# Batch 0 of an attention and expert kernel: float32 probabilities, joint weight scales, other priorities

## The chip, the cores and the metric

The kernel runs on one core of a Trainium2 chip. The metric is device time in microseconds (us), as the median of the runs. A core has five engines that work side by side, each through its own instructions in a fixed order: TensorE (PE, matmuls; the loads of its stationary operand are listed as PEld), VectorE (DVE), ScalarE (ACT), GpSimd (POOL) and SyncE (SP), which here only issues DMA transfers. They wait for each other by semaphores.

## The reference

Causal attention over 4 batches of 12 heads, 448 positions of 64 columns, and behind it an expert layer whose hidden values are the largest of three products:

```python
scores = scale * np.matmul(q, k.transpose(0, 1, 3, 2))
scores = np.where(mask, -1000000000.0, scores)
scores = scores - np.max(scores, axis=-1, keepdims=True)
attn = np.exp(scores)
attn = attn / (np.sum(attn, axis=-1, keepdims=True) + 1e-09)
attn_out = np.matmul(attn, v)
x = attn_out.transpose(0, 2, 1, 3).reshape(1792, 768)
h = np.maximum(np.maximum(x @ w1, x @ w2), x @ w3)
out = h @ w_out
```

All four weight matrices are 768 x 768 and arrive in float64; q, k and v are float32.

## The kernel before, in words

**Number formats.** Expert and output products run in float16 with each operand split in two parts, a high one (the value rounded) and a low one (what is left): three matmuls, high x high, high x low, low x high, stand for one in higher precision. Splitting costs a copy for the high part and a subtraction for the low part (`scaled`, `rest`, `scaled_rest`, lines 306 to 331, so that many rows of the profile carry L308, L312, L319 or L328).

**Attention** goes by pairs of heads, six to a batch, 24 in all (`attend`, line 432). A pair has two halves of blocks. For each half TensorE computes masked scores into PSUM (tile S, line 449, in float32), VectorE takes maxima (L476), ScalarE exponentiates with a running sum (L487) into tile p. Then ScalarE adds a small number to the sums (L496), VectorE takes reciprocals (L499), ScalarE multiplies every block by its reciprocal (L308, p<-p), makes the high part (L308, ph<-p), and VectorE or GpSimd the low part (L319). A DMA transposes both parts to tile pT (L549), issued by SP. For the first pair alone (`ON_PE = 1`) TensorE transposes instead (L517), and ScalarE and VectorE copy the two parts out of PSUM. The product with v is 60 float16 matmuls into tile O (L569), which ScalarE or VectorE and VectorE split into x (L308 or L310, L328).

**Values** (line 362): v of a batch is loaded to tiles vr, its largest absolute value found (L378 or L376), spread over partitions by a matmul against the identity and a maximum (`all_max`, L344 and L347), and v scaled by a power of two into high and low part.

**Weights** (line 593): 24 tiles, three (one of each of w1, w2, w3) for each of six slices f, and six of w_out. A tile is loaded into one of two staging buffers wst (L603). ScalarE takes the absolute value of the high words (L634), VectorE clamps and takes the maximum (L619), and puts the float64 bits together as float32 in three steps (L623, L627, L631). A power of two as its scale comes from a chain of its own: L344 on TensorE, then L347, L644, L649, L357, L657 on VectorE. With it the tile is split into high and low part (L308 or L312, L328). For each f the ratios of the three scales are found (L675 to L677); when the last tile's scale is known, tile wu (L685).

**Experts** (lines 701 and 752): for batch b and slice f, 54 float16 matmuls (L715), whose three results VectorE and ScalarE bring to a common scale and take the largest of (L308, L729); then the projection (L761) and the output.

**Order.** The instructions are not issued as the functions are written. Each function adds operations with a cost, the names that they read and write, a ring of buffers and a priority to a planner (`Order`, line 54). It plays the program through with the costs and puts each operation on an engine where it can start first, by priority among those ready, and the code is issued in that sequence. Pair u has priority 10 u, weight tile m priority 10 W_AT[m] + 5, the experts 5000 and up. The table `ENGINES` says which engines may take a kind of operation, `RINGS` how many buffers each kind has. What the planner gives is a fixed order on each engine.

Of the kernel before, what the change touches and what calls it, by code (L numbers as in the profile page):

```python
# [30 lines left out]
W_AT = [2.0, 2.3, 2.6, 2.9, 3.2, 3.5, 3.8, 4.1, 4.4, 4.7, 5.0, 5.3, 5.6, 5.9, 6.2, 6.5, 6.8, 7.1, 8.0, 8.3, 8.6, 8.9, 9.2, 9.5]  # L31
V_AHEAD = 2

ON_PE = 1
ENGINES = {
    "q": ("pool", "act"), "v max": ("act",), "v hi": ("act", "pool"), "v lo": ("dve", "pool"), "p": ("act",),
    "p hi": ("act",), "p lo": ("dve", "pool"), "t hi": ("act",), "x hi": ("act", "dve"),
# [4 lines left out]
    qr=3, kr=3, acc=2, p32=2, ph=3, pT=2, v16=5, vr=4, x=4, wst=2, w3=2, h=6, hacc=4, osb=2, S=2, O=1, M=3)  # L42
# [214 lines left out]
def attention_moe(ctx: ExitStack, tc: tile.TileContext, q, k, v, w1, w2, w3, wo, out):  # L257
# [9 lines left out]
        pT=([P, 16, P], F16), v16=([P, 2, DM], F16), vr=([P, DM], F32), x=([P, 3, 2, S_LEN], F16), wst=([P, 3072], F16),  # L267
        w3=([P, DM], F32), h=([P, 2, S_LEN], F16), hacc=([P, S_LEN], F32), osb=([P, HF], F32))
# [5 lines left out]
    tiny = c1.tile([P, 1], F32, name="tiny")  # L274
# [6 lines left out]
    oscL = c1.tile([P, 1], F32, name="oscL")  # L281
    osc = c1.tile([P, 4], F32, name="osc")
# [8 lines left out]
    wx = c1.tile([P, 24], F32, name="wx")  # L291
# [67 lines left out]

    VROWS = [(j, P if j < 3 else 64) for j in range(4)]  # L360

    def values(b, prio):

        s, name = bsc[:, b], ("scale", b)
        for j, n in VROWS:
            t = ("vr", b, j)

            def ld(e, j=j, t=t, n=n):
                ENG[e].dma_start(T(t)[0:n], v[b, P * j : P * j + n, :])

            add(c_dma((n, 3072)), ld, writes=[t], ring=("vr", t), prio=prio)


            def sm(e, j=j, t=t, n=n):
                if e == "act":
                    ACT.activation(junk[0:n, 0:DM], T(t)[0:n], AF.Abs, accum_out=s[0:n, j : j + 1])  # L376
                else:
                    DVE.tensor_reduce(  # L378
                        out=s[0:n, j : j + 1], in_=T(t)[0:n], op=ALU.max, axis=AX.X, apply_absolute_value=True)

            c = dict(act=c_act(DM, 0.09), dve=c_dve(DM))
            add([(e, c[e]) for e in (("dve",) if b == 0 else ENGINES["v max"])], sm, reads=[t], writes=[("sum", b, j)], prio=prio)
# [9 lines left out]
        f = s[:, 10:11]  # L392
        for j, n in VROWS:
            t, v16 = ("vr", b, j), ("v16", b, j)
            first = b == 0 and j == 3
# [36 lines left out]
    def attend(b, p, prio, on_pe):  # L432
# [4 lines left out]
        for z, blocks in enumerate(HALVES):  # L437
# [56 lines left out]

            def eps(e, cols=cols):
                ACT.activation(cols(14), cols(7), AF.Identity, bias=tiny, scale=1.0 / PS)  # L496
# [12 lines left out]

            if on_pe:  # L510

                for g in range(2):
                    M, t = ("M", "t", b, p, z, g), pT[z]

                    def tr(e, g=g, M=M, y=y):
                        for i in range(4):
                            PE.transpose(T(M)[:, i * P : i * P + P], T(y)[:, (4 * g + i) * P : (4 * g + i + 1) * P], ident)  # L517

                    def place(t, g, pl):
                        return T(t)[:, 8 * pl + 4 * g : 8 * pl + 4 * g + 4].rearrange("p a b -> p (a b)")  # L520

                    def t_hi(e, g=g, M=M, t=t):
                        scaled(e, place(t, g, 0), T(M)[:, 0:512], 1.0)

                    def t_lo(e, g=g, M=M, t=t):
                        rest(e, place(t, g, 1), T(M)[:, 0:512], place(t, g, 0))

                    own = [(y, bl[0]) for bl in blocks if any(512 * g <= bl[3] + 512 * k < 512 * g + 512 for k in range(bl[2]))]
                    add([("pe", 0.5)], tr, reads=own, writes=[M], ring=("M", M), prio=pr + 0.4)
                    c = dict(act=c_act(512), dve=c_dve(512))  # L530
                    add([(e, c[e]) for e in ENGINES["t hi"]], t_hi, reads=[M], writes=[(t, 0, g)],
                        ring=("pT", t) if g == 0 else None, prio=pr + 0.4, bank=M, chain=t)
                    add([("dve", c["dve"])], t_lo, reads=[M, (t, 0, g)], writes=[(t, 1, g)], prio=pr + 0.4, bank=M)
                continue
# [25 lines left out]
        def pv(e):  # L560
# [11 lines left out]

        vb = [(("v16", b, j), z) for j in range(4) for z in range(2)]
        add([("pe", 3 * c_pe(*(6 * [P] + 4 * [D])) + 0.3)], pv, reads=[(pT[z], pl, g) for z in range(2) for pl in range(2) for g in range(2)] + vb, writes=[O],
            ring=("O", O), prio=prio + 0.9)
        x, kx = ("x", b, p // 3), p % 3
        fx = 1.0 / PS

        def x_hi(e):
            scaled(e, T(x)[:, kx, 0], T(O)[:, 0:S_LEN], fx)  # L580
# [12 lines left out]
    def weight(m, prio):  # L593
# [234 lines left out]
    for m in range(24):  # L828
        weight(m, 10 * W_AT[m] + 5)
# [39 lines left out]
```

## Time and profile before

| | |
|---|---|
| median of 3 runs | 527.47 us (527.2 to 531.83) |
| the profiled execution: span from first to last instruction | 525.1 us |
| TensorE busy in it | 477.4 us, 91% |
| VectorE, ScalarE, GpSimd busy | 308.1, 318.7, 116.7 us |
| 16 DMA engines, mean share | 52.7% of the span, 65.03 MB |

The profile is of one execution, for which the span is given; the runs of the median were timed without it. [...] The granted clock is given as a share of full speed.

### The profile page before, as it was taken

How to read it: one execution, taken by the hardware profiler on the slowest of the kernel's cores; microseconds unless marked ns; L12 is line 12 of the kernel's file. 1: busy time of each engine (PE TensorE's matmuls, PEld its weight loads, DVE VectorE, ACT ScalarE, POOL GpSimd, SP SyncE). 2: the span in 40 equal slices, each digit the busy share in tenths (PEclk: the TensorE clock that was granted, in tenths of full speed). 3: DMA queues.
4: the chain of work that ended last, by engine and by line, in shares of the span. 5: the costliest groups of instructions: out<-in, count | busy, mean ns of one | idle time of the engine just before them, and what ended most of it. 6: DMA issues, size and time to landing. Idle time of an engine off the chain costs nothing.

```text
span 525.1 us, 9862 instructions
## 1 busy us (share of the span) xinstructions
PE 477.4 (91%) x3826; PEld 279.3 (53%) x3826; DVE 308.1 (59%) x609; ACT 318.7 (61%) x768; POOL 116.7 (22%) x115
## 2 busy tenths in 40 slices
PE   6767554799999999998999999999999999999996
PEld 3445433446555555554665556665555555555563
DVE  5889998999999997995556856333212200212200
ACT  3999688778979879589999797582110111110111
POOL 3432334515556556030021210000000000000000
PEclk9766857799999999999999999999999999999999
DMA  7787797876987998843787840665200011000012
GB/s 233 216 227 180 163 250 205 248 166 169 223 166 212 205 195 176 230 83 79 159 177 145 147 81 12 133 150 104 48 0 1 1 45 46 0 1 0 1 62 60
DMA packets 127599, 65.66 MB, mean 125 GB/s; under 512 B 101440, under 2 KB 124992, under 8 KB 127552
## 3 DMA queue, kind: packets, MB, share of 16 engines
q1 hardware_dynamic: 127552, 65.03, 52.7%
q8 instruction: 30, 0.49, 0.4%
q14 instruction: 17, 0.14, 0.1%
HBM read 35.39 MB, written 5.51 MB: 78 GB/s over the span
## 4 chain that ended last, share of the span: by engine, by line
PE 55%; DVE 21%; ACT 15%; DMA 6%; issue 3%; SPq 0%; ACTq 0%; DVEq 0%
PE M L715 31%; PE M L761 13%; PE S L449 7%; ACT p L487 3%; ACT p L308 3%; DVE w L627 3%; PE O L569 3%; DVE acc L476 2%; ACT ph L308 2%; DVE w L619 2%; ACT w L308 2%; DMA vr<-in_v_dram 2%; DVE w L631 2%; DMA wst<-in_moe_w_dram 2%; ACT w L634 2%
## 5 line engine op out<-in xcount | busy, mean ns | idle before, releaser
L715 PE MATMUL M<-x,w 128*128 128x448 f16 x1296 | 254.7, 355 | 0.0
L715 PEld LDWEIGHTS <-w 128*128 128x128 f16 x1296 | 125.4, 98 | 118.0 <-issue 6.3
L729 DVE SCALAR_TENSOR_TENSOR hacc<-M,wr,hacc 128x448 f32<-128x448 f32 x48 | 32.7, 681 | 105.5 <-PE M L715 105.5
L487 ACT ACTIVATE p<-S,acc 128x384 f32<-128x384 f32 (+3 forms) x168 | 82.9, 500 | 16.2 <-DVE acc L476 7.6
L308 ACT ACTIVATE p<-p,acc 128x384 f32<-128x384 f32 (+3 forms) x168 | 78.1, 531 | 17.4 <-DVE acc L499 16.9
L449 PE MATMUL S<-kr,qr 64*128 64x384 f32 (+4 forms) x384 | 74.9, 446 | 0.0
L761 PE MATMUL M<-w,h 128*128 128x384 f16 x432 | 72.1, 326 | 0.0
L476 DVE TENSOR_REDUCE acc<-S 128x2 f32<-128x512 f32 (+2 forms) x96 | 62.3, 680 | 15.9 <-PE S L449 15.6
L319 POOL TENSOR_TENSOR ph<-p,ph 128x1024 f16<-128x1024 f32 x25 | 56.6, 2266 | 63.2 <-ACT ph L308 46.7
L308 ACT ACTIVATE h<-hacc 128x448 f16<-128x448 f32 x24 | 13.6, 577 | 72.4 <-DVE hacc L729 72.3
L449 PEld LDWEIGHTS S<-kr,qr 64*128 64x128 f32 (+1 forms) x384 | 45.2, 211 | 21.9 <-issue 14.8
L761 PEld LDWEIGHTS <-h 128*128 128x128 f16 x432 | 41.6, 98 | 28.5 <-issue 1.0
L745 POOL COPY hL<-h 128x128 f16<-128x128 f16 x24 | 9.7, 407 | 208.0 <-DVE h L319 207.8
L308 ACT ACTIVATE ph<-p 128x1024 f16<-128x1024 f32 x46 | 48.3, 1051 | 0.5 <-DMA pT<-ph 0.3
L569 PEld LDWEIGHTS <-v 128*64 128x64 f16 x1440 | 39.1, 119 | 10.8 <-issue 10.5
L569 PE MATMUL O<-pT,v 128*64 128x128 f16 (+1 forms) x1440 | 41.9, 221 | 2.7 <-DMA pT<-ph 2.7
L319 DVE TENSOR_TENSOR ph<-p,ph 128x1024 f16<-128x1024 f32 x21 | 25.7, 1222 | 17.0 <-ACT ph L308 15.0
L449 PE MATMUL S<-mk,identb 128*128 128x128 bf16 (+1 forms) x120 | 19.2, 263 | 17.0 <-ACT p L487 10.7
L487 ACT ACTIVATION_READ_ACCUMULATOR p<-S,acc 128x1 f32 x168 | 34.2, 204 | 0.0
L308 ACT ACTIVATE osb<-M,osc 128x384 f32<-128x384 f32 x22 | 12.8, 580 | 30.6 <-PE M L761 30.5
L308 ACT ACTIVATE hacc<-M,wr 128x448 f32<-128x448 f32 x24 | 15.2, 634 | 26.4 <-PE M L715 26.4
L344 PE MATMUL M<-ident,wmx 128*128 128x128 f32 x48 | 13.1, 360 | 17.7 <-DVE w L619 17.7
(79 smaller groups left out, 410.5 us busy)
## 6 DMA issues: line engine op xcount, KB each, us to landing
wst<-in_moe_w_dram SPq DMA_DIRECT2D x18, 768.0 KB, 5.0
kr<-in_k_dram SPq DMA_DIRECT2D x24, 224.0 KB, 3.3
qr<-in_q_dram SPq DMA_DIRECT2D x24, 192.0 KB, 3.7
vr<-in_v_dram SPq DMA_DIRECT2D x12, 384.0 KB, 4.8
wst<-in_moe_w_out_dram SPq DMA_DIRECT2D x6, 768.0 KB, 5.7
out_dram<-osb SPq DMA_DIRECT2D x24, 192.0 KB, 1.9
qr<-in_q_dram SPq DMA_DIRECT2D x48, 16.0 KB, 3.3
vr<-in_v_dram SPq DMA_DIRECT2D x4, 192.0 KB, 4.9
```

Of the source, the lines that this page charges most:

```text
L308: ACT.activation(o, i, AF.Copy, scale=f)
L319: ENG[eng].tensor_tensor(out=o, in0=i, in1=hi, op=ALU.subtract)
L344: PE.matmul(T(M)[:, i * P : i * P + P], ap(c, 0, [[0, P]]), ident, start=True, stop=True)
L449: PE.matmul(o[:, c : c + w], l, r, start=start, stop=True, skip_group_check=True)
L476: DVE.tensor_reduce(out=T(acc)[:, at : at + len(g)], in_=i, op=ALU.max, axis=AX.XY if parts == 2 else AX.X, negate=True)
L487: ACT.activation(part(T(y), parts, c, w), part(T(S), parts, c, w), AF.Exp, bias=T(acc)[:, at : at + 1], accum_out=T(acc)[:, 7 + at : 8 + at])
L569: PE.matmul(T(O)[D * h : D * h + D, P * i : P * i + w], vt[j][:, vl, (2 * p + h) * D : (2 * p + h + 1) * D], T(pT[u])[:, 8 * pl + c, a : a ...
L619: DVE.tensor_scalar(out=T(x32), in0=T(x32), scalar1=MIN_HI, scalar2=None, op0=ALU.max, op1=ALU.max, accum_out=wmx[:, c])
L627: DVE.scalar_tensor_tensor(out=xi(), in0=word(0), scalar=29, in1=xi(), op0=ALU.logical_shift_right, op1=ALU.bitwise_or)
L715: PE.matmul(T(M)[:, 0:S_LEN], w16[j][:, kk, wl, fs], xx[:, kk % 3, xl], start=(kk == 0 and wl + xl == 0), stop=(kk == 5 and wl == 1))
L729: DVE.scalar_tensor_tensor(out=a, in0=ps, scalar=r, in1=a, op0=ALU.mult, op1=ALU.max)
L761: PE.matmul(T(M)[:, 0:HF], lhs(f, hl), w16[3][:, f, wl, es], start=(f == 0 and hl + wl == 0), stop=(f == 5 and hl == 1))
```

## The change

**Batch 0 in float32** (`PLAIN = 6`, all pairs of batch 0). v of batch 0 is loaded as float32 straight into the buffers of the two float16 parts and not split. For its six pairs the exponentials stay as they are: no normalization, no split. TensorE transposes them in float32 (four groups of four transposes), ScalarE or VectorE copies each group from PSUM to pT. The product with v is 20 float32 matmuls. The reciprocals of the sums are spread over the head's 64 partitions by eight matmuls against the identity into one of the three PSUM tiles M, copied with v's scale to a tile of the ring hacc, and the product is multiplied by them on VectorE (line 623 of the new code); then x is split. The transposes by DMA remain for batches 1 to 3.

**Scales.** For three weight tiles there is one chain: three matmuls side by side in one tile M, one maximum with three results, and four small steps on three columns.

**Priorities and tables.** W_AT has other numbers; the maxima of v of batch 0 may go to ScalarE or VectorE, the low part of x of batch 0 to VectorE or GpSimd, the copies to pT and of the reciprocals to ScalarE or VectorE.

```diff
-W_AT = [2.0, 2.3, 2.6, ..., 9.2, 9.5]
+W_AT = [1.0, 1.2, 1.39, ..., 6.13, 6.32]
-ON_PE = 1
+PLAIN = 6
+FIRST = 1
...
+            if plain:
+                for g in range(2):
+                    M, t = ("M", "t", b, p, z, g), pT[z]
+                    def tr(e, g=g, M=M, y=y):
+                        for i in range(4):
+                            PE.transpose(T(M)[:, i * P : i * P + P], T(y)[:, (4 * g + i) * P : (4 * g + i + 1) * P], ident)
+                    def place(e, g=g, M=M, t=t):
+                        scaled(e, raw(t)[:, 512 * g : 512 * g + 512], T(M)[:, 0:512], 1.0)
...
+                continue
...
+        def pv_plain(e):
+            vt = [raw(("v16", b, j)) for j in range(4)]
...
+                        PE.matmul(
+                            T(O)[D * h : D * h + D, P * i : P * i + w], vt[j][:, (2 * p + h) * D : (2 * p + h + 1) * D],
+                            raw(pT[u])[:, a : a + w], start=n_ == 0, stop=n_ == len(per[0]) - 1)
...
+            def reciprocals(e):
+                a = T(acc)
+                DVE.tensor_scalar(out=a[:, 14:21], in0=a[:, 7:14], scalar1=1e-9, scalar2=None, op0=ALU.add)
+                DVE.reciprocal(a[:, 21:28], a[:, 14:21])
+            def spread(e):
...
+                        PE.matmul(
+                            T(R)[D * h : D * h + D, P * i : P * i + P], ap(a, 21 + (2, 4, 0)[i] + h, [[0, D]]), ident,
+                            start=True, stop=True)
...
+            def quotient(e):
+                DVE.tensor_tensor(out=T(x32), in0=T(O)[:, 0:S_LEN], in1=T(x32), op=ALU.mult)
...
-        all_max(("wt", m), [wmx[:, c]], pm, [("wmx", m)], [("wt", m)], prio)
...
+    def scales(f, prio):
+        c, names = slice(3 * f, 3 * f + 3), [("wt", 3 * f + z) for z in range(3)]
+        pm, tt, ff = wpm[:, c], wt[:, c], wf[:, c]
+        all_max(("wt", f, "all"), [wmx[:, 3 * f + z : 3 * f + z + 1] for z in range(3)], pm, [("wmx", 3 * f + z) for z in range(3)],
+                names, prio)
...
-            attend(b, p, 10 * u + 2, u < ON_PE)
+            attend(b, p, 10 * u + 2, u < PLAIN)
...
-    for m in range(24):
-        weight(m, 10 * W_AT[m] + 5)
+    for f in range(8):
+        for m in range(3 * f, 3 * f + 3):
+            weight(m, 10 * W_AT[m] + 5)
+        scales(f, 10 * W_AT[3 * f + 2] + 5)
+        for m in range(3 * f, 3 * f + 3):
+            split(m, 10 * W_AT[m] + 5)
```

**What the planner makes of it.** On VectorE, during batch 0, one weight tile's own scale chain before (w_91 and w_92 are buffers of weights, wpm, wx, wt and wf the columns of the scale, S_105 scores of the next half):

```order
L328 SCALAR_TENSOR_TENSOR w_0_111<-w_91,wf,w_0_111 128x6x128
L627 SCALAR_TENSOR_TENSOR w_92<-wst_90,w_92 128x768
L347 TENSOR_REDUCE wpm<-M_108 128x1
L476 TENSOR_REDUCE acc_68<-S_105 128x2
L644 TENSOR_SCALAR wx<-wpm 128x1
L649 SCALAR_TENSOR_TENSOR wt<-wpm,wx 128x1
L357 TENSOR_SCALAR wt<-wt 128x1
L657 RECIPROCAL wf<-wt 128x1
```

and the first joint chain in the new order (acc_67 holds the sums and reciprocals of a pair, w_87 is the third tile of the group):

```order
L347 TENSOR_REDUCE wpm<-M_111 128x3
L689 SCALAR_TENSOR_TENSOR w_87<-wst_92,w_87 128x768
L712 TENSOR_SCALAR wt<-wpm 128x3
L693 SCALAR_TENSOR_TENSOR w_87<-wst_92,w_87 128x768
L354 TENSOR_SCALAR wt<-wt 128x3
L608 TENSOR_SCALAR acc_67<-acc_67 128x7
L609 RECIPROCAL acc_67<-acc_67 128x7
L357 TENSOR_SCALAR wt<-wt 128x3
L497 TENSOR_REDUCE acc_68<-S_106 128x2
L719 RECIPROCAL wf<-wt 128x3
```

The five steps stand once for three tiles, with three columns each, between the same bit steps and score maxima.

On ScalarE, the end of the second pair of batch 0 before (p_69 and p_70 are the halves' exponentials, ph their float16 parts):

```order
L308 ACTIVATE p_69<-p_69,acc_68 128x384 x2
L308 ACTIVATE p_69<-p_69,acc_68 128x128 x2
L308 ACTIVATE p_70<-p_70,acc_68 128x256
L308 ACTIVATE ph_71<-p_69 128x1024
L308 ACTIVATE p_70<-p_70,acc_68 128x256
L308 ACTIVATE p_70<-p_70,acc_68 128x2x256
L308 ACTIVATE x_85<-O_107 128x448
L308 ACTIVATE ph_72<-p_70 128x1024
```

and the same pair in the new order (M_109 to M_111 are PSUM tiles with transposed probabilities or, into hacc, spread reciprocals):

```order
L508 ACTIVATE p_70,acc_68<-S_107,acc_68 128x256 x2
L308 ACTIVATE x_88<-hacc_100 128x448
L508 ACTIVATE p_70,acc_68<-S_107,acc_68 128x2x256
L308 ACTIVATE pT_74<-M_109 128x512
L395 ACTIVATE junk,bsc<-vr_81 128x768
L308 ACTIVATE pT_75<-M_110 128x512
L308 ACTIVATE pT_75<-M_109 128x512
L308 ACTIVATE hacc_101<-M_111,bsc 128x448
```

The normalizations and the float16 parts are gone, and copies out of PSUM stand in their place.

On SP, the transfers about the second and third pair before:

```order
L603 DMA wst_89<-in_moe_w_dram 128x6x256
L549 DMA_TRANSPOSE pT_74<-ph_71 128x16x128
L549 DMA_TRANSPOSE pT_75<-ph_72 128x16x128
L423 DMA kr_66<-in_k_dram 128x448
L418 DMA qr_63<-in_q_dram 128x384
L420 DMA qr_63<-in_q_dram 64x64 x2
```

and in the new order:

```order
L665 DMA wst_92<-in_moe_w_dram 128x6x256
L376 DMA vr_84<-in_v_dram 64x768
L444 DMA kr_66<-in_k_dram 128x448
L439 DMA qr_63<-in_q_dram 128x384
L441 DMA qr_63<-in_q_dram 64x64 x2
L665 DMA wst_93<-in_moe_w_dram 128x6x256
```

No transposes stand between the loads of batch 0; the first is for the first pair of batch 1.

## Rows read from the trace of the kernel before

**Rows 1.** Chain of work that ended last: start, length, what.

```profile
262.60 0.68 ACT p L487 x2
...
439.40 57.89 PE M L715 x306
497.29 23.41 PE M L761 x144
```

**Rows 2.** Page, 40 slices: granted clock of TensorE in tenths.

```profile
PEclk9766857799999999999999999999999999999999
```

**Rows 3.** Windows: stretch, length; busy PE, PEld, DVE, ACT, POOL; clock, DMA share, GB/s.

```profile
0.00:99.70 99.70, 63.66 (x582) 42.34 (x582) 86.46 (x191) 77.10 (x200) 36.32 (x44) 0.74 0.81 212
99.70:232.20 132.50, 127.17 (x1056) 73.18 (x1057) 125.14 (x261) 110.35 (x262) 61.69 (x42) 0.97 0.81 192
...
23.00:26.40 3.40, 3.28 (x26) 2.04 (x26) 3.40 (x7) 3.40 (x12) 0.00 (x0) 0.50 0.79 206
```

**Rows 4.** Timeline of VectorE, and one piece of GpSimd's: start, length, what.

```profile
22.75 2.85 DVE L328 SCALAR_TENSOR_TENSOR v<-vr,bsc,v 128x768 f16<-128x768 f32 x3
...
30.31 0.62 DVE L328 SCALAR_TENSOR_TENSOR x<-O,x 128x448 f16<-128x448 f32 x1
...
99.68 0.61 DVE L328 SCALAR_TENSOR_TENSOR x<-O,x 128x448 f16<-128x448 f32 x1
...
101.08 6.62 DVE L328 SCALAR_TENSOR_TENSOR v<-vr,bsc,v 128x768 f16<-128x768 f32 x3
...
101.69 5.21 POOL L319 TENSOR_TENSOR ph<-p,ph 128x1024 f16<-128x1024 f32 x2 [0.38 <-ACT ph L308]
...
232.11 1.20 DVE L685 TENSOR_TENSOR wu<-wt,wtm 128x6 f32<-128x6 f32 x1
```

**Rows 5.** Groups by line: engine, operation, tiles, shapes, count; busy, mean ns; idle.

```profile
L347 DVE TENSOR_REDUCE wpm<-M 128x1 f32<-128x128 f32 x24 | 6.8, 281 | 0.9 <-PE M L344 0.8
L644 DVE TENSOR_SCALAR wx<-wpm 128x1 int32<-128x1 int32 x24 | 3.5, 144 | 0.1
L649 DVE SCALAR_TENSOR_TENSOR wt<-wpm,wx 128x1 int32<-128x1 int32 x24 | 11.8, 493 | 0.1
L357 DVE TENSOR_SCALAR wt<-wt 128x1 f32<-128x1 f32 x24 | 3.5, 147 | 0.2
L657 DVE RECIPROCAL wf<-wt 128x1 f32<-128x1 f32 x24 | 3.8, 156 | 0.1
...
L619 DVE TENSOR_SCALAR_CACHE_REDUCE w<-w 128x768 f32<-128x768 f32 x24 | 22.7, 946 | 5.4 <-ACT w L634 5.4
L623 DVE TENSOR_SCALAR w<-w 128x768 int32<-128x768 int32 x24 | 14.5, 602 | 0.0
L631 DVE SCALAR_TENSOR_TENSOR w<-wst,w 128x768 int32<-128x768 int32 x24 | 23.5, 977 | 0.0
L328 DVE SCALAR_TENSOR_TENSOR w<-w,wf,w 128x768 f16<-128x768 f32 x24 | 24.3, 1011 | 1.0 <-ACT w L308 1.0
...
L319 DVE TENSOR_TENSOR ph<-p,ph 128x1024 f16<-128x1024 f32 x21 | 25.7, 1222 | 17.0 <-ACT ph L308 15.0 <-issue 2.0
L328 DVE SCALAR_TENSOR_TENSOR v<-vr,bsc,v 128x768 f16<-128x768 f32 x11 | 13.1, 1210 | 1.0 <-POOL v L312 1.0
L378 DVE TENSOR_REDUCE bsc<-vr 128x1 f32<-128x768 f32 x3 | 2.8, 949 | 5.0 <-DMA vr<-in_v_dram 5.0
...
L308 ACT ACTIVATE p<-p,acc 128x384 f32<-128x384 f32 (+3 forms) x168 | 78.1, 531 | 17.4 <-DVE acc L499 16.9
L308 ACT ACTIVATE ph<-p 128x1024 f16<-128x1024 f32 x46 | 48.3, 1051 | 0.5 <-DMA pT<-ph 0.3
```

**Rows 6.** Timeline of TensorE: start, length, what.

```profile
16.77 1.62 PE L517 MATMUL M<-ident,p 128*128 128x128 f32 x12
...
279.26 1.57 PE L569 MATMUL O<-pT,v 128*64 128x128 f16 x60
...
281.09 1.14 PE L449 MATMUL S<-kr,qr 64*128 64x384 f32 x8
```

More of the change, by code (lines that the diff above doesn't have):

```diff
@@ L392, in values @@
         f = s[:, 10:11]
+        if plain(b):
+            return
         for j, n in VROWS:
             t, v16 = ("vr", b, j), ("v16", b, j)
-            first = b == 0 and j == 3
+            first = b == FIRST and j == 3
             if first:
@@ L508, in attend @@
                     port=True)
[L510 to L534, printed above, removed]
             def p_hi(e, z=z, y=y):
@@ L579, in x_hi @@
+        add([("pe", 3 * c_pe(*(6 * [P] + 4 * [D])) + 0.3)], pv, reads=pb + vb, writes=[O],
+            ring=("O", O), prio=prio + 0.9)
         def x_hi(e):
@@ new lines, in scales, with ratios @@
+        add([("dve", 0.15)], lambda e: exponent(tt, tt), writes=names, prio=prio)
+        add([("dve", 0.15)], lambda e: at_least(tt, 2.0**-62), writes=names, prio=prio)
+        add([("dve", 0.15)], lambda e: DVE.reciprocal(ff, tt), reads=names, writes=[("wf", 3 * f + z) for z in range(3)], prio=prio)
+        if f < KC:
+            def ratios(e):
+                DVE.tensor_reduce(out=wtm[:, f : f + 1], in_=tt, op=ALU.max, axis=AX.X)
+                DVE.reciprocal(wtm[:, 6 + f : 7 + f], wtm[:, f : f + 1])
+                DVE.tensor_scalar(
+                    out=wr[:, c], in0=tt, scalar1=wtm[:, 6 + f : 7 + f], scalar2=2.0**-18, op0=ALU.mult, op1=ALU.mult)
+            add([("dve", 0.5)], ratios, reads=names, writes=[("wr", f), ("wtm", f)], prio=prio + 1)
@@ L659, in place, with split @@
+    def split(m, prio):
+        x32, ff = ("w32", m), wf[:, m : m + 1]
+        f, j = divmod(m, 3) if m < 18 else (m - 18, 3)
         def place(hl):
@@ L670, in weight @@
             reads=[("wf", m), ("w", m, 0)], writes=[x32, ("w", m)], prio=prio, port=True)
-        if m < 18 and j == 2:
-            t3 = wt[:, 3 * f : 3 * f + 3]
-            def ratios(e):
-                DVE.tensor_reduce(out=wtm[:, f : f + 1], in_=t3, op=ALU.max, axis=AX.X)
-                DVE.reciprocal(wtm[:, 6 + f : 7 + f], wtm[:, f : f + 1])
-                DVE.tensor_scalar(
-                    out=wr[:, 3 * f : 3 * f + 3], in0=t3, scalar1=wtm[:, 6 + f : 7 + f], scalar2=2.0**-18,
-                    op0=ALU.mult, op1=ALU.mult)
-            add([("dve", 0.5)], ratios, reads=[("wt", m - z) for z in range(3)], writes=[("wr", f), ("wtm", f)], prio=prio)
         if m == 23:
```

98 lines of the change are left out of this document (68 added, 30 removed).

## Prediction

> **What bounds the kernel now.** I read the profile from the end backwards. In the chain of work that ended last the last piece of another engine that matters is ScalarE's at 262.60 us; behind it stand only scores, products, expert matmuls and projections, at the end two pieces of 57.89 and 23.41 us [rows 1]. So the last half is TensorE's own work, and only an earlier beginning helps. The page's line of the granted clock says where TensorE is not full: in the first quarter slices lie below full speed [rows 2]. The windows show the same by stage [rows 3]: up to 99.7 us TensorE is busy 63.66 us at a mean clock of 0.74, while VectorE is busy 86.46 of 99.7 us; then 127.17 of 132.5 us, beside VectorE at 125.14.
>
> What ends the first stage is VectorE. Its timeline shows the last x of batch 0 written at 99.68 us [rows 4]; only then can the 1296 expert matmuls run on, since each sums over all twelve heads. VectorE stays the second bound until 232.11 us, where the last weight's scale is known (tile wu).
>
> So the time is: start of the experts, plus a rest of TensorE's work that the change leaves alone (the order before and after has the scores of eight pairs of heads and six products with v ahead of the first expert matmul, and all else behind it), plus what the weights hold it up. I predict the shift of the start and of the wu instruction.
>
> **The change part by part.** The base is the profiled execution's span, 525.1 us; the median of the runs is 527.47, 2.4 more, and I add the gain to that.
>
> *VectorE up to the last x of batch 0.* Summed along its own order with the mean durations of this trace, VectorE has 101.1 us of instructions there before and 71.2 after. The pieces, from [rows 5]:
> - Scales: nine chains of 281 + 144 + 493 + 147 + 156 = 1221 ns (11.0 us) become two chains for three tiles each. The maximum over 384 columns is not in the trace; between 281 ns for 128 and 946 for 768 I put it at 547, and the four small ones at 147 each: 1.1 us a chain, 2.3 in all. Saved 8.7.
> - The low parts of the probabilities: four on VectorE at 1222 ns, saved 4.9. The low parts of v of batch 0: four at 1210, saved 4.8. Three maxima of v at 949 go to ScalarE: 2.8.
> - Added: per pair two reciprocal steps and one product, less the old reciprocals and the old x: 0.3 together.
> - Not saved but moved behind the start: the four steps of one weight (946 + 602 + twice 977), two low parts of weights (2 x 1011), a low part of v, a set of ratios and two maxima of scores, about 9.
>
> Together -30. Before, the 74.2 us of durations between the first pair's x (30.31) and the last (99.68) took 69.4 us, a factor 0.935, as neighbours overlap a little. After, pair 0 should end near 21 us (scores, four exponentials, transposes, product in a chain) with 13.2 us of durations done, and 58.0 are left: 21 + 0.935 x 58.0 = 75.
>
> *VectorE from there to wu.* The sums are 139.1 before, which took 132.4 us (0.952), and 142.9 after, as the moved 9 us come back and the remaining chains are cheaper. With 136 us the wu instruction falls 136 us behind the start.
>
> *TensorE in the first stage.* 47 us at full clock (63.66 x 0.74) stand there now, an upper bound as latency counts as busy. Added for five pairs are 16 transposes: twelve took 1.62 us [rows 6], so 0.135 each, 2.16 a pair. The product with v in float32 has 20 matmuls, 2048 columns over both heads. The float32 scores of 1024 such columns took 1.14 us [rows 6], so 2.3 us; spreading the reciprocals, 896 columns, 1.0 us; the 1.57 us of the float16 product goes. That is 3.9 a pair, less the transposes that pair 0 has already: 6 x 3.9 - 2.2 = 21 us. No row shows float32 with 64-column weights. From below: if its columns cost what those of the float16 product do, a third of 1.57 and 0.2, the sum is 6 us. From above: if the two heads don't run beside each other, twice the price, 41 us. I take 21, the float32 row being the nearest. The hidden stage then needs 68 us at full clock.
>
> *ScalarE.* Per pair of batch 0 it loses seven normalizations at 531 ns, two high parts at 1051 and two small ones (some 6.4 us), and gets about 3.3 copies of 512 columns, one of the spread reciprocals and a maximum of v, at 531 to 949 each: some 3.5 to 4.5. It was busy 77.10 of 99.7 us; about 65 remain. With VectorE at 71 and TensorE at 68 three engines are now loaded nearly alike, and each waits in order for the others. For that I add 6 us to VectorE's 75: the experts start at 81 instead of 99.7, a shift of 18.7. The bounds are 75 (VectorE packed as before) and 96 (TensorE's upper price of 41 us, 88 us from some 8 us on).
>
> *Contention.* Three low parts of v took 6.62 us from 101.08, with GpSimd in a tensor_tensor of 5.21 us over them, where three took 2.85 us at 22.75 [rows 4]. [...] The 493 ns of L649, beside 144 for L644 on as many columns, look like the same wait, as L649 has two inputs in SBUF [rows 5]; the new chain has no such step. The change gives GpSimd five of the low parts of x, about 1 us each, and takes four low parts of p from VectorE. I cost it at nothing to +5 us, within the 6 us of waits.
>
> *Transfers.* The ten transposes by DMA of pairs 1 to 5 vanish from SP's queue ahead of the start. The DMA share there was 0.81 and the chain is VectorE's, so I count nothing; if a weight now lands late, VectorE waits in order with everything behind it, which the rival on weights prices. The new priorities leave the weights about where they stood beside the pairs: eight are staged on VectorE by the start, nine before.
>
> *Sum.* The start says 18.7 us. The wu instruction says 81 + 136 = 217 instead of 232.1, so 15. TensorE stands at wu one pair's attention further and one expert block less, so neither bound decides alone; I take 17: 527.5 - 17 = 510.5 us. The likeliest case's own range is 504 to 518.
>
> **The rivals.**
> *TensorE's clock stays low, and the added float32 work makes it the bound (slower).* Place: the first stage. [...] At 0.74 the 68 us become 92 and end near 100, no gain at all; at 0.65 they become 105 and end at 113, 13 us later than before: 540. It decides from a mean clock below about 0.73 on with no gaps at all, or below 0.8 with 8 us of gaps. Against: where work lay close, from 99.7 on, the mean was 0.97. [...]
>
> *The weights become the bound.* The start moves, but VectorE, with 3.8 us more between start and wu than before, waits for loads or for ScalarE as well. Then only 5 to 10 us are left: 517 to 522.5. For: VectorE was 94% busy there. Against: the loads land as before, with ten transposes fewer beside them.
>
> *No change.* The in-order queues of three engines loaded alike give back nearly all: the start at 95 to 100, so 523 to 530.
>
> *All packs.* The start at 75 and wu at 211, the 21 us full: 506 less what the DMA's freed share returns; 498 to 504.
>
> **How the numbers follow.** The forecast has 0.61, the weights 0.17, no change 0.08, slower 0.06, all packs 0.08. The range from 502 to 523 leaves out the slower rival, half of "no change" and part of "all packs". About 1% (5 us) is what a measurement of this kernel can tell from no change. Faster by over 1%, below 522.2: 0.61 + 0.08 + nearly all of 0.17 = 0.85. Within 1%: 0.09. Slower: 0.06.
>
> **What would show it.** Right: the last x of batch 0 near 81 us, wu near 217, the chain from about 245 on TensorE alone, VectorE's busy time down by some 25 us from 308, a clock over 0.85 up to 81 us. Wrong: a float32 product with v well over 2.3 us, a clock near 0.74 with TensorE full in the first stage, or a start near 80 and wu later than 225.

## The result, and the profile after

The changed kernel takes 514.62 us (median of 4 runs, 513.25 to 516.43); the kernel before, run on the same chip, 527.75 us (4 runs). The ratio is 0.9742 with an interval of 0.9705 to 0.9778, so 13.1 us less. The profiled execution has a span of 512.7 us, 12.4 less than before, at a mean granted clock of 0.983 instead of 0.943.

The page of the changed kernel: busy time, share of the span and instructions of each engine, then the granted clock in 40 slices, which answers to [rows 2].

```profile
PE 481.5 (94%) x3882; PEld 288.7 (56%) x3882; DVE 290.6 (57%) x519; ACT 303.9 (59%) x735; POOL 102.6 (20%) x109
...
PEclk9789899999999999999999999999999999999999
```

TensorE has 4.1 us more busy time and stands at a higher clock; VectorE has 17.5 us less. The digits 6, 6, 8, 5, 7, 7 of slices 3 to 8 have become 8, 9, 8, 9, 9, 9.

VectorE's timeline has the two events that the prediction followed: the last product of batch 0 (its x is split from it) and the wu instruction [rows 4].

```profile
80.62 0.62 DVE L623 TENSOR_TENSOR hacc<-O,hacc 128x448 f32<-128x448 f32 x1
...
224.46 0.14 DVE L749 TENSOR_TENSOR wu<-wt,wtm 128x6 f32<-128x6 f32 x1
```

The second was at 232.11 and is at 224.46 us. The first is not quite the event of before: there the low part of the last x was VectorE's, at 99.68 us, and here it comes behind the product, on GpSimd:

```profile
82.00 1.03 POOL L319 TENSOR_TENSOR x<-hacc,x 128x448 f16<-128x448 f32 x1 [1.49 <-ACT x L308]
```

So the start is 19.1 us earlier by the product and 17.7 by the low part of x. I go by the product below. TensorE's timeline has its next expert matmul behind these events at 101.80 us before and at 85.37 now, 16.4 us earlier. The windows cut at the product and at the wu instruction answer to [rows 3] (stretch, length; busy PE, PEld, DVE, ACT, POOL; clock, DMA share, GB/s):

```profile
0.00:80.60 80.60, 65.70 (x606) 49.79 (x607) 62.68 (x131) 58.34 (x154) 23.21 (x37) 0.89 0.62 195
80.60:224.50 143.90, 132.85 (x1165) 78.12 (x1165) 138.09 (x243) 125.73 (x306) 54.55 (x38) 1.00 0.81 189
224.50:512.70 288.20, 282.97 (x2114) 160.75 (x2112) 89.81 (x147) 119.88 (x276) 24.85 (x34) 1.00 0.28 61
```

Busy time times granted clock I take as TensorE's work at full clock: 65.70 x 0.89 = 58.5 us in the first stage here. In the kernel before, eight score matmuls on 64x384 took 2.08 us from 23.64 us on, at a clock of 0.50, and as many 1.14 us from 281.09 on, at 1.00. Matmuls that lie close overlap in it: the 306 of L779 in the chain below take 57.88 us together, 189 ns each, where each is listed with 352 ns in the median. What is left of the stretch, 80.6 - 58.5 = 22.1 us, I call its shortfall: idle time and what the low clock costs. Before, the three stretches have 52.6, 9.1 and 6.4 us of shortfall and 457.0 us of work; now 22.1, 11.1 and 5.2 us, and 474.3 us of work. So the first stage gave 30.5 us, the third 1.2, the second took 2.0 back, and 17.3 us of new work were paid from that: 30.5 + 1.2 - 2.0 - 17.3 = 12.4, the change of the span. The low slices of the page were worth more than the change cost, and the one stage that lost something is the second.

The chain of work that ended last answers to [rows 1] (start, length, what). Its last pieces before TensorE alone:

```profile
222.03 1.90 DVE wt L712
...
225.03 0.55 DVE wu L752
...
231.30 3.04 ACT w L308 x2
234.34 1.26 ACT p L508 x6
235.60 0.04 issue
235.64 1.45 PE S L470 x10
...
426.93 57.88 PE M L779 x306
484.81 23.41 PE M L825 x144
```

From 235.64 us on it is TensorE's own, where that began at 263.28 (262.60 + 0.68) before. And a step on three numbers per partition, L712, stands in it with 1.90 us. The groups of the joint chain and of the two bit steps with two inputs answer to [rows 5]:

```profile
L319 POOL TENSOR_TENSOR ph<-p,ph 128x1024 f16<-128x1024 f32 x19 | 42.1, 2216 | 56.2 <-ACT ph L308 28.2 <-issue 27.3 <-POOL ph L319 0.8
...
L689 DVE SCALAR_TENSOR_TENSOR w<-wst,w 128x768 int32<-128x768 int32 x24 | 25.2, 1056 | 0.1
L693 DVE SCALAR_TENSOR_TENSOR w<-wst,w 128x768 int32<-128x768 int32 x24 | 24.6, 1029 | 0.0
...
L712 DVE TENSOR_SCALAR wt<-wpm 128x3 int32<-128x3 int32 x8 | 5.8, 724 | 0.0
...
L347 DVE TENSOR_REDUCE wpm<-M 128x3 f32<-128x384 f32 x8 | 4.4, 551 | 0.4 <-PE M L344 0.4
...
L354 DVE TENSOR_SCALAR wt<-wt 128x3 int32<-128x3 int32 x8 | 3.2, 401 | 0.0
...
L357 DVE TENSOR_SCALAR wt<-wt 128x3 f32<-128x3 f32 x8 | 3.1, 383 | 0.0
...
L719 DVE RECIPROCAL wf<-wt 128x3 f32<-128x3 f32 x8 | 1.3, 162 | 0.0
```

The maximum over 384 columns takes 551 ns, as estimated (547). The three tensor_scalar steps take 724, 401 and 383 ns instead of 147. The reciprocal beside them, as small, takes 162. The timeline shows what they wait for (start, length, engine, line):

```profile
109.36 2.37 POOL L319 TENSOR_TENSOR ph<-p,ph 128x1024 f16<-128x1024 f32 x1 [1.48 <-issue]
...
110.34 1.42 DVE L712 TENSOR_SCALAR wt<-wpm 128x3 int32<-128x3 int32 x1
...
138.87 0.16 DVE L712 TENSOR_SCALAR wt<-wpm 128x3 int32<-128x3 int32 x1
...
139.13 2.13 POOL L319 TENSOR_TENSOR ph<-p,ph 128x1024 f16<-128x1024 f32 x1 [4.37 <-ACT ph L308]
139.27 2.02 DVE L354 TENSOR_SCALAR wt<-wt 128x3 int32<-128x3 int32 x1
```

GpSimd's low part of the probabilities ran until 111.73 (109.36 + 2.37), and L712, begun at 110.34, until 111.76; the next until 141.26, and L354 until 141.29. Each time the small step ends 0.03 us behind GpSimd's instruction; so does the L712 of the chain above, at 223.93. In between, at 138.87 with no such instruction running, the same L712 takes 0.16 us.

### The profile page after: what moved, and what is told of

The parts are those of the page before. It is cut to its first block, busy times and chain, and to the rows that moved or that the text cites. A ratio compares the mean times of both kernels' runs of the same rounds, so it can differ in the third digit from the quotient of the medians.

```text
span 512.7 us, 9828 instructions
## 1 busy us (share of the span) xinstructions
PE 481.5 (94%) x3882; PEld 288.7 (56%) x3882; DVE 290.6 (57%) x519; ACT 303.9 (59%) x735; POOL 102.6 (20%) x109
## 4 chain that ended last, share of the span: by engine, by line
PE 57%; DVE 23%; ACT 11%; issue 4%; DMA 3%; SPq 1%; ACTq 0%; DVEq 0%
PE M L779 31%; PE M L825 16%; PE S L470 5%; DVE acc L497 4%; ACT p L508 3%; DVE w L689 3%; PE O L582 3%; ACT p L308 3%; DVE w L693 2%; DVE w L328 2%; DMA wst<-in_moe_w_dram 2%; DVE w L681 2%; ACT ph L308 1%; DMA v<-in_v_dram 1%; ACT w L696 1%
## 5 line engine op out<-in xcount | busy, mean ns | idle before, releaser
L779 PE MATMUL M<-x,w 128*128 128x448 f16 x1296 | 251.7, 353 | 2.7 <-DVE w L328 1.6
L779 PEld LDWEIGHTS <-w 128*128 128x128 f16 x1296 | 124.1, 98 | 120.0 <-issue 3.6
L793 DVE SCALAR_TENSOR_TENSOR hacc<-M,wr,hacc 128x448 f32<-128x448 f32 x48 | 32.6, 680 | 115.0 <-PE M L779 114.9
L497 DVE TENSOR_REDUCE acc<-S 128x2 f32<-128x768 f32 (+1 forms) x96 | 62.2, 680 | 19.2 <-PE S L470 17.4
L470 PE MATMUL S<-kr,qr 64*128 64x384 f32 (+4 forms) x384 | 67.0, 406 | 0.0
L308 ACT ACTIVATE p<-p,acc 128x384 f32<-128x384 f32 (+3 forms) x126 | 58.9, 532 | 12.1 <-DVE acc L538 12.1
L319 POOL TENSOR_TENSOR ph<-p,ph 128x1024 f16<-128x1024 f32 x19 | 42.1, 2216 | 56.2 <-ACT ph L308 28.2
L470 PEld LDWEIGHTS S<-kr,qr 64*128 64x128 f32 (+1 forms) x384 | 40.7, 190 | 18.5 <-issue 10.6
L308 ACT ACTIVATE ph<-p 128x1024 f16<-128x1024 f32 x36 | 37.8, 1051 | 0.7 <-DMA pT<-ph 0.6
L319 DVE TENSOR_TENSOR ph<-p,ph 128x1024 f16<-128x1024 f32 x17 | 20.8, 1222 | 16.2 <-ACT ph L308 15.2
L582 PEld LDWEIGHTS <-v 128*64 128x64 f16 x1080 | 26.3, 111 | 5.8 <-issue 5.6
L582 PE MATMUL O<-pT,v 128*64 128x128 f16 (+1 forms) x1080 | 28.3, 210 | 0.0
L689 DVE SCALAR_TENSOR_TENSOR w<-wst,w 128x768 int32<-128x768 int32 x24 | 25.2, 1056 | 0.1
```

The source lines that it names most:

```text
L308: ACT.activation(o, i, AF.Copy, scale=f)
L319: ENG[eng].tensor_tensor(out=o, in0=i, in1=hi, op=ALU.subtract)
L470: PE.matmul(o[:, c : c + w], l, r, start=start, stop=True, skip_group_check=True)
L497: DVE.tensor_reduce(out=T(acc)[:, at : at + len(g)], in_=i, op=ALU.max, axis=AX.XY if parts == 2 else AX.X, negate=True)
L582: PE.matmul(T(O)[D * h : D * h + D, P * i : P * i + w], vt[j][:, vl, (2 * p + h) * D : (2 * p + h + 1) * D], T(pT[u])[:, 8 * pl + c, a : a ...
L689: DVE.scalar_tensor_tensor(out=xi(), in0=word(0), scalar=29, in1=xi(), op0=ALU.logical_shift_right, op1=ALU.bitwise_or)
```

## The experiments

Ratios are against the kernel before, run beside them on the same chip: 529.02 us for the three kernels on the wait behind GpSimd, 528.5 for the next four, 526.93 for the last four. So a difference of 1 or 2 us between two groups says nothing. The table gives for each kernel the stages of its profiled execution, worked out from the windows as above; weight tiles are the clamps that VectorE's timeline has ahead of the start of the experts. The work comes out as 457 or 474 us within some 4 us, whatever the order (the clock has only two digits); what differs is the shortfall. The start is a point of VectorE's work: the product of the last pair where batch 0 is in float32, else the low part of its x. TensorE's next expert matmul comes 0.6 to 8.0 us behind it, 8.0 in the kernel without priorities (at 89.59 us).

| kernel | median us | weight tiles ahead of the start | start, us | wu, us | TensorE's work | shortfall by stage |
|---|---|---|---|---|---|---|
| before | 527.75 | 9 | 99.7 | 232.1 | 457.0 | 52.6, 9.1, 6.4 |
| after | 514.62 | 8 | 80.6 | 224.5 | 474.3 | 22.1, 11.1, 5.2 |
| single columns | 511.06 | 8 | 82.2 | 221.0 | 475.7 | 22.1, 7.7, 4.5 |
| GpSimd in quarters | 510.10 | 8 | 79.2 | 219.6 | 475.1 | 19.6, 8.6, 4.8 |
| both | 507.18 | 8 | 81.4 | 216.2 | 474.6 | 21.9, 4.2, 4.4 |
| without float32 | 538.51 | 11 | 114.9 | 249.2 | 457.1 | 66.7, 8.8, 5.9 |
| without joint chain | 546.45 | 14 | 114.9 | 206.6 | 476.3 | 54.5, 5.9, 7.5 |
| without priorities | 527.43 | 8 | 81.6 | 238.7 | 473.1 | 24.3, 20.0, 8.0 |
| float32 alone | 539.69 | 11 | 97.0 | 204.4 | 470.1 | 39.8, 13.3, 14.3 |
| joint chain alone | 550.92 | 8 | 101.8 | 263.4 | 457.0 | 54.1, 20.6, 16.9 |
| priorities alone | 536.36 | 12 | 114.5 | 232.5 | 460.2 | 64.1, 5.9, 4.9 |
| both, weights earlier | 514.78 | 8 | 80.9 | 225.0 | 474.0 | 22.4, 11.6, 5.1 |
| both, weights later | 515.41 | 8 | 78.9 | 219.1 | 474.3 | 19.3, 12.9, 4.7 |

### The wait behind GpSimd

Three kernels hold the order of the changed one and touch only the suspected wait. The first gives the steps of the joint chain to VectorE column by column:

```diff
-            DVE.tensor_scalar(out=tt.bitcast(I32), in0=pm.bitcast(I32), ...)
+            for z in range(3):
+                DVE.tensor_scalar(out=tt[:, z : z + 1].bitcast(I32), in0=pm[:, z : z + 1].bitcast(I32), ...)
...
-        lambda e: exponent(tt, tt)
+        lambda e: [exponent(tt[:, z : z + 1], tt[:, z : z + 1]) for z in range(3)]
```

and likewise the lower bound (L357) and the ratios (L725).

> The changed kernel with the same order of instructions; only the small steps of a joint weight scale (L712, L354, L357 and the last step of the ratios) work on three single columns, one after the other, instead of on three columns at once. Theory A: these three-column steps are where VectorE waits for GpSimd's low parts of p, 8.4 us in all between the start of the experts and wu (L712 alone 4.5 us above its shortest); single columns do not wait, so the steps fall to about 0.15 us each, wu comes 3 to 6 us earlier than 224.5 and the median is 509 to 512. Rival B: the wait only passes to the next two-input step of VectorE behind it, wu stays within 2 us of 224.5, and with two more instructions a step the median is 514 to 518. Rival C: VectorE's waits go, but TensorE or ScalarE sets the time there: wu earlier, the median still 513 to 516.

Measured: 511.06 us (509.07 to 512.65), ratio 0.9658 [0.9608, 0.9708], wu at 221.03. The groups of this kernel (columns as above):

```profile
L713 DVE TENSOR_SCALAR wt<-wpm 128x1 int32<-128x1 int32 x24 | 2.2, 145 | 0.0
L354 DVE TENSOR_SCALAR wt<-wt 128x1 int32<-128x1 int32 x24 | 2.1, 143 | 0.0
L357 DVE TENSOR_SCALAR wt<-wt 128x1 f32<-128x1 f32 x24 | 2.1, 143 | 0.0
```

Three times as many instructions take less time, 6.4 us instead of 12.1. 38 of the 72 run from start to end inside a tensor_tensor of GpSimd's, and the longest of all takes 0.15 us: these steps don't wait on one column. Between start and wu VectorE's six chains (maxima and reciprocals included) took 15.4 us in the changed kernel and take 9.1 here. The waits did not pass to the bit steps with two inputs, as rival B has it: there L689 and L693 lie 4.9 us above their shortest in the changed kernel and 4.7 here.

The second cuts GpSimd's low part of the probabilities into four instructions of 256 columns and leaves the joint chain alone:

```diff
-                rest(e, t[:, 1024:2048], T(y), t[:, 0:1024])
+                n = 4 if e == "pool" else 1
+                for i in range(n):
+                    g = slice(1024 // n * i, 1024 // n * (i + 1))
+                    rest(e, t[:, 1024:2048][:, g], T(y)[:, g], t[:, 0:1024][:, g])
```

> The changed kernel with the same order of instructions; only GpSimd's low parts of p are made in four instructions of 256 columns instead of one of 1024. Theory A (VectorE waits for the end of the GpSimd instruction that runs, whichever step it is): single waits of VectorE fall from up to 2.9 us to under 1.6, the sum of its lengths above the shortest of each form between start and wu from 21 us to 8 to 14, wu from 224.5 to 214 to 220, median 506 to 511. Rival B: the four pieces follow each other so closely that VectorE waits for all four: lengths as before, median 514 to 516. Rival C: the pieces cost GpSimd so much more that the low parts come late: one low part over 2.6 us, median over 516.

Measured: 510.10 us (509.86 to 510.34), ratio 0.9642 [0.96, 0.9684], wu at 219.63. Its groups:

```profile
L319 POOL TENSOR_TENSOR ph<-p,ph 128x256 f16<-128x256 f32 x76 | 52.1, 716 | 52.1 <-ACT ph L308 30.4 <-issue 20.7 <-POOL qr L312 1.0
...
L715 DVE TENSOR_SCALAR wt<-wpm 128x3 int32<-128x3 int32 x8 | 2.5, 308 | 0.0
```

GpSimd is busy 10 us longer with the same work (76 x 716 ns against 19 x 2216), and still the kernel is faster: a wait now ends with one quarter, and no tensor_scalar of the joint chain takes over 0.60 us, where the longest took 2.02. A low part takes 2.74 us of GpSimd, over the 2.6 that were to mark rival C, but the time is theory A's. The longest wait that I find in VectorE's timeline between start and wu, as duration over the shortest of the same form, falls from 1.96 to 0.78 us, and the sum of all that lies over the shortest from 18.9 to 11.9. Of the joint chain it is the first step that gains (724 to 308 ns, the others 401 to 391 and 383 to 323); the two bit steps with two inputs fall from 4.9 to 1.4 us above their shortest.

The third has both edits.

> Both edits of the two runs before at once, same order of instructions. Theory A: the gains add up partly, since both take away the same waits: median 505 to 510, not more than 2 us below the better one of the two. Rival B: neither does anything, 514 to 518.

Measured: 507.18 us (506.86 to 507.95), ratio 0.9592 [0.9541, 0.9642], the fastest of all: 7.4 us below the changed kernel, and the wu instruction at 216.22 us, where the prediction had it. The two edits add nearly whole (3.6 and 4.5 us alone), where at most 2 us below the better one were expected and 2.9 came.

### Which part of the change gives the gain

Here the kernels are planned anew, since the planner sees other operations or priorities. So each run shows what a part is worth together with the order made for it, not in an order held fixed.

Without float32: the kernel before with joint scales and the new W_AT. It also has a third buffer for a weight in float32 (ring w3, two before), as the changed kernel has: a tile of the group holds one until the joint scale is known. That buffer was not tried alone.

```diff
-W_AT = [2.0, 2.3, 2.6, ..., 9.2, 9.5]
+W_AT = [1.0, 1.2, 1.39, ..., 6.13, 6.32]
...
+        scales(f, 10 * W_AT[3 * f + 2] + 5)
```

> The kernel before with the joint scales (and the third buffer w3 that they need) and the new priorities, but with batch 0 in two float16 parts as before. Theory: the shift of the start of the experts, from 99.7 to 80.6 us, is mostly the float32 batch 0, as it takes some 30 us of VectorE's and ScalarE's work and ten transposes by DMA away; without it the start falls back to 92 to 98 and the median is 520 to 526. Rival: the joint scales alone give the start (8.7 of the 30 us of VectorE's work): start at 85 to 91, median 514 to 519.

Measured: 538.51 us, ratio 1.0197 [1.0149, 1.0245], slower than before and outside both expectations. The new numbers put 11 instead of 9 weight tiles ahead of the start, which falls at 114.9 us. VectorE is busy 99.24 of these 114.9 us; that the tiles brought forward push batch 0's attention back is my reading of that.

Without the joint chain: the changed kernel with a chain for each tile.

```diff
-        scales(f, 10 * W_AT[3 * f + 2] + 5)
...
+        all_max(("wt", m), [wmx[:, c]], pm, [("wmx", m)], [("wt", m)], prio)
```

> The changed kernel with one scale chain for each weight tile, as before, and the new priorities and the float32 batch 0 kept. Theory: the joint chain saves small steps but keeps the wait for GpSimd, so undoing it costs VectorE about 1 us a tile in the first stage and less behind it: start at 84 to 90, wu at 226 to 234, median 515 to 521. Rival: the joint chain is worth nothing as the wait moved with it: median 512 to 515.

Measured: 546.45 us, ratio 1.0341 [1.0281, 1.04], far outside both expectations. The order has 14 tiles ahead of the start (114.9 us), where the changed kernel has 8; I take them for the time that batch 0 lost. That a tile with a chain of its own can be split at once, while the joint chain holds three back until the last has come, is what I read from the code as the reason; it was not tried by itself.

Without priorities: the changed kernel with the old W_AT.

```diff
-W_AT = [1.0, 1.2, 1.39, ..., 6.13, 6.32]
+W_AT = [2.0, 2.3, 2.6, ..., 9.2, 9.5]
```

> The changed kernel with the old table W_AT. Theory: the priorities only shift weights against pairs and the planner keeps VectorE full either way: median within 1% of 514.6, 510 to 520. Rival: with the old table the weights come after the pairs, wu falls behind and the experts wait for weights: median 521 to 530.

Measured: 527.43 us (525.66 to 531.35, 10 runs), ratio 0.9984 [0.9951, 1.0017]. The time and the late wu are the rival's. The start comes at 81.6 us, 18 us earlier than before, and yet nothing is gained.

The windows of this kernel between start and wu:

```profile
81.60:238.70 157.10, 144.31 (x1238) 85.29 (x1239) 144.14 (x248) 128.71 (x316) 63.97 (x46) 0.95 0.74 185
```

and what TensorE waited for from 81 to 240 us (engine, tile and line; us in total, times, longest):

```profile
PE S L470 <- ACT p L508: 6.8, 5, 3.2
PE S L470 <- DMA wst<-in_moe_w_dram: 3.8, 1, 3.8
```

VectorE is idle for 13.0 of 157.1 us there (5.8 of 143.9 in the changed kernel), the clock is 0.95, and wu comes at 238.7. The shortfall grows by 8.9 us in this stage and by 2.8 behind it.

Float32 alone: the changed kernel with a chain for each tile and the old W_AT (both edits as above). The third buffer of w3 and the new tables stay.

> The kernel before with the float32 batch 0 alone (one scale chain for each tile, old table W_AT). Theory: the float32 batch 0 brings most of the 13 us: median 515 to 521, start at 80 to 88. Rival: without the cheaper scales VectorE has no room and the start gains little: median 522 to 528.

Measured: 539.69 us, ratio 1.0235 [1.0177, 1.0293], outside both expectations. The weights are done at 204.4 us, but batch 1 is late. TensorE's timeline shows it (in brackets the idle time before and what ended it):

```profile
194.89 0.48 PE L470 MATMUL S<-mk,identb 128*128 128x128 bf16 x3 [4.67 <-ACT p L508]
...
205.82 0.53 PE L582 MATMUL O<-pT,v 128*64 128x128 f16 x6 [4.26 <-DMA pT<-ph]
```

TensorE waits 4.67 us for exponentials and 4.26 for a transposition of probabilities, about the time at which the last weight's scale is known (204.4): the weights are early and the attention late.

The joint chain alone, in the kernel before:

> The kernel before with the joint chain for three weight tiles alone (and the third buffer that goes with it). Balance theory: what counts is how many weight tiles the order puts on VectorE ahead of the last x of batch 0, and how many pairs are through when the last weight's scale is known. Here 8 tiles stand ahead of the start (9 before) and 14 pairs ahead of wu (13 before), as in the changed kernel, with batch 0's old work: so the start falls a little earlier than 99.7 us (92 to 99), wu at 228 to 236, and the time within 1.5% of before, 520 to 532 us. Rival, the joint chain alone is the gain: start below 92, under 516 us. Second rival, no part is good without the others: over 534 us.

Measured: 550.92 us, ratio 1.0446 [1.0384, 1.0508]: the second rival's result, and my theory of the number of tiles ahead of the start is wrong here. The number was 8 as foreseen, yet the start is at 101.8 and wu at 263.4. VectorE is idle for 18.1 of the 161.6 us between them, where it was for 7.4 of 132.5 before.

The priorities alone, in the kernel before:

> The kernel before with the new numbers of W_AT alone. Balance theory: 12 weight tiles stand ahead of the last x of batch 0 instead of 9, and 12 pairs ahead of wu instead of 13: the start falls some 15 us later (110 to 118), wu earlier (205 to 222), and the time is longer than before, 532 to 545 us, as TensorE waits for pairs. Rival, an earlier wu is worth its time whatever the start: under 524 us.

Measured: 536.36 us, ratio 1.0170 [1.0098, 1.0242]. The start (114.5 us) and the time are as expected, wu (232.5) is 10 us later than the range.

No part by itself is a gain, and without any one the gain is gone, each in the order that was planned for it.

### How steep the priorities are

The fastest kernel, with all numbers of W_AT times 0.9:

```diff
-W_AT = [1.0, 1.2, 1.39, ..., 6.13, 6.32]
+W_AT = [0.9, 1.08, 1.25, ..., 5.52, 5.69]
```

> The kernel with both edits (three single columns, GpSimd's low parts in four instructions; 507.18 us) with all numbers of W_AT times 0.9. The order has 8 tiles ahead of the start as there, and 20 instead of 19 ahead of the last x of batch 1. Balance theory: near its best place, so within 1% of 507 us (502 to 512), wu at 211 to 217. Rival, the weights are still the bound after 81 us and more of them earlier helps further: under 502 us. Second rival, the place is steep, as the run with the old numbers (12.8 us) suggests: over 512 us.

and times 1.1 (1.1, 1.32, 1.53, ..., 6.74, 6.95):

> The same kernel with all numbers of W_AT times 1.1 (the old numbers were about 1.5 times the new at the end). Balance theory: within 1% of 507 us (502 to 512), wu at 215 to 222. Rival, the cost of late weights grows from the first step on: 512 us or more.

Measured: 514.78 us (ratio 0.9759 [0.9704, 0.9814]) and 515.41 (0.9763 [0.9702, 0.9824]), so 7.6 and 8.2 us over 507.18 on both sides; not within 1%; the rivals that have the place steep, over 512 us, were right. The loss is in the second stage, 11.6 and 12.9 us of shortfall against 4.2. TensorE's waits from 80 to 260 us, in the fastest kernel,

```profile
PE S L470 <- ACT p L508: 1.5, 4, 0.8
PE M L785 <- DVE w L328: 0.9, 1, 0.9
```

with the weights earlier,

```profile
PE S L470 <- ACT p L508: 6.8, 6, 2.4
PE M L785 <- DVE w L328: 3.0, 2, 1.8
```

and with them later:

```profile
PE O L585 <- DMA pT<-ph: 3.0, 1, 3.0
PE S L470 <- ACT p L508: 2.9, 4, 0.9
```

They are other waits each time, some for attention and some for weights. So an order planned anew for a shift of the priorities by a tenth moves the time by about 8 us, and of the results of the section before, only differences well over 8 us can be put down to the part that was left out, together with its order. That is so for the joint chain (32 us with float32 batch 0, in the wrong direction without it) and for float32 batch 0 (24 us). The 12.8 us of the priorities are near it. What each part is worth by itself is not shown.

## Why the prediction was right or wrong

It was 510.5 us with a range of 502 to 523, and the time is 514.62: a right forecast, with one term priced at about half of what it took and some luck in how the two shifts were put together.

*The start, 81 us: right (80.62 by the product, 82.00 by the low part of x).* VectorE's durations up to and with the product come to 71.2 us, as predicted. Pair 0 ended 2 us later (its product at 23.09 us), and the rest took 57.5 us where 54 and 6 of waits were predicted. The clock is 0.89 up to the start, over the 0.85 that was asked, so the rival of a low clock fell: TensorE was neither full (65.70 of 80.6 us) nor at 0.74. TensorE's work there is 58.5 us at full clock, where 68 was put as an upper bound; ScalarE is busy 58.34 us where some 65 were expected. So the three engines were loaded less alike than the 6 us of waits were argued from. The clocks of 0.73 and 0.8 from which the rival was to decide give an end at 93 us by its own 68; to hold 81 it asks for 0.84, or 0.93 with 8 us of gaps. Over the span the added work is 17.3 us where 21 was taken.

*The stretch at a clock of 0.50* [rows 3] has its first matmul at 23.12 us, behind 2.33 us in which TensorE was idle:

```profile
23.12 0.59 PE L449 MATMUL S<-mk,identb 128*128 128x256 bf16 x2 [2.33 <-ACT p L487]
```

What lowers the clock there is not shown.

*The float32 pair.* The groups of the transposes and of the product (columns as above; the trace has two records for each of the 20 products of a pair):

```profile
L522 PE MATMUL M<-ident,p 128*128 128x128 f32 x96 | 16.3, 312 | 6.2 <-ACT p L508 5.7 <-ACT hacc L308 0.4
...
L595 PE MATMUL O<-pT,v 128*64 128x128 f32 x144 | 11.1, 313 | 5.3 <-DVE hacc L623 5.3
...
L595 PE MATMUL O<-pT,v 128*64 128x64 f32 x96 | 4.6, 250 | 0.0
```

Six products have 15.7 us, 2.6 a pair, and six times 16 transposes 2.7 a pair; at the stage's clock of 0.89 these are 2.3 and 2.4 us at full clock, as against 2.3 and 2.16 predicted. With 80 transposes more than before, in between products and scores, the clock of the stage rose from 0.74 to 0.89. What transposes by themselves do to the clock is not shown: no run here has them alone.

*The wu instruction 136 us behind the start: wrong, it is 143.9.* This is the step that failed: "the four small ones at 147 each", and beside it "the new chain has no such step". The chain was priced 547 + 4 x 147 = 1135 ns and takes 551 + 724 + 401 + 383 + 162 = 2221. The six chains between start and wu take 15.4 us and not 6.8, so 8.6 too much. All of VectorE's durations there come to 154.7 us where 142.9 were predicted, 11.8 more: beside the chains the two bit steps with two inputs are 3.9 us above their mean of before, the low parts of v 2.0 below it. As neighbours overlap a little more (143.9 of 154.7, a factor of 0.930), 7.9 us of error are left. I had read the 493 ns of L649 rightly as a wait behind GpSimd, but took two inputs to be its only condition. Of the 24 in the kernel before, the ten that begin while GpSimd is in a tensor_tensor take 0.24 to 1.49 us and end within 0.03 us of its end; the others take 0.14 to 0.16. The trace of the kernel before had a step on three columns, which the price left aside:

```profile
L677 DVE TENSOR_SCALAR wr<-wt,wtm 128x3 f32<-128x3 f32 x6 | 3.4, 569 | 0.2
```

Two of the six take 0.23 us; the four that begin while GpSimd is in a tensor_scalar on 128x768 take 0.73 to 0.74, and each ends 0.01 to 0.02 us behind it. On single columns (the kernel of that name) the same step takes 0.2 us; three at a time take 0.45 to 0.46 us, four of the six groups inside such an instruction:

```profile
L727 DVE TENSOR_SCALAR wr<-wt,wtm 128x1 f32<-128x1 f32 x18 | 2.7, 208 | 0.2
```

So it is the number of columns, not the second operand, that makes this step wait. The other steps agree: of the 24 tensor_scalar on 128x3 in the joint chains of the changed kernel, the six that begin while GpSimd is in a tensor_tensor take 0.77 to 2.02 us and the other 18 take 0.12 to 0.20; on 128x1 they took 143 to 145 ns on the mean. Why three columns wait and one does not is not shown. Single columns bring the chains to 9.1 us, the stage to 138.8 and the time to 511.06, so 5.1 of the 7.9 us are shown to be these steps; with GpSimd's piece shortened as well, the stage takes 134.8 us and wu stands at 216.22, the predicted 217. The sign of being wrong, a wu later than 225, was missed by half a us.

*The gain as a middle of the shift of the start and of wu: close, but by luck.* The two moved by 19.1 and 7.6 us, whose middle, 13.3, is close to the measured 13.1. In other kernels the same rule fails: float32 alone moves them by 2.7 and 27.7 us, a middle of 15.2, and its span is 12.4 us longer than before; without the joint chain the middle is 5.2 and the span 19.1 us longer. The rule leaves out what comes behind wu and the 17.3 us of new work, which the account by shortfall has in it.

*VectorE's busy time down by 25: it is 17.5.* The same error: 8 chains x (2221 - 1135) = 8.7 us. With single columns it is 24.3 (308.1 to 283.8).

*TensorE alone from about 245 us: it is 235.64,* earlier than thought, though wu is later. The prediction gives no working for it. The distance from wu was 31.2 us before (263.28 - 232.11) and is 11.2 now, and this is part of the 1.2 us that the third stage gave, no more: the work in between is TensorE's anyway.

*"The new priorities leave the weights about where they stood", counted at nothing: not borne out.* I had counted tiles ahead of the start (8 and 9). With the old numbers the start is within 1 us and the count the same, but wu comes at 238.7 instead of 224.5 and the time is 527.43. The priorities place the weights behind the start, which I didn't look at. The rival on weights had the place, wu, and 517 to 522.5 us; the result lies between it and the forecast. It did not have the mechanism: VectorE was to wait for loads or for ScalarE, but between start and wu it is idle for 5.8 us, and was for 7.4 before. Its instructions themselves lasted longer.

*Transfers at nothing:* the DMA share fell from 0.81 to 0.62 in the first stage; nothing here shows a gain by that, and it wasn't tried alone.

Left open is why the joint chain alone loses 24 us at the same number of tiles ahead of the start, and which instruction makes the time so steep in W_AT on both sides; the waits shown are its place, not its cause.

## What to carry to other kernels

Account for the bounding engine by stages, as work at full clock and shortfall: here the work stayed within some 4 us of 457 or 474 over thirteen kernels, and each result could be read from the shortfall of its stages. A merged small step is cheaper by its count only if it doesn't wait where the single one didn't (here 724, 401 and 383 ns on three columns, 143 to 145 on one): look for the shape at which an operation begins to wait for another engine, and in the trace at hand for a step that has the shape already. Where a planner sets the order, test a suspected wait in an order held fixed, and change priorities by a tenth first to learn how much the order alone moves the time.

## What the runs showed of the hardware

In the changed kernel each tensor_scalar of the joint chains on 128x3 that began while GpSimd was in a tensor_tensor ended 0.02 to 0.03 us behind it (six of 24, 0.77 to 2.02 us; the others 0.12 to 0.20). In the kernel with single columns those on 128x1 did not wait (143 to 145 ns on the mean over 72 instructions, 38 of them inside one of GpSimd's). Cutting GpSimd's 2216 ns instruction into four of 716 cost GpSimd 10 us (42.1 to 52.1 busy) and gave the kernel 4.5 (514.62 to 510.10).

Six pairs of float32 transposes, products and scores in the first stage ran at a granted clock of 0.89, higher than the 0.74 of the float16 version, in which TensorE was idle for 36.0 of 99.7 us where it is now for 14.9 of 80.6. The number format by itself did not raise it: the kernel without the joint chain has the same float32 pairs, with TensorE idle for 35.5 of 114.9 us and a clock of 0.76:

```profile
0.00:114.90 114.90, 79.41 (x614) 56.57 (x615) 96.05 (x229) 64.35 (x157) 24.79 (x40) 0.76 0.55 167
```
